# Loading the last 96 rows of w_out in two transfers of eight lanes

## The chip, the cores and the metric

The kernel runs on one core of a Trainium2 chip. The metric is the device time of one execution in microseconds (us). The core has five engines with queues of their own (TensorE, VectorE, ScalarE, GpSimd, SyncE) and sixteen DMA engines, which carry out the transfers that SyncE and ScalarE issue here.

## The reference

One decode step for a batch of four: a normalised input goes through attention over a cache of 4096 positions and, beside it, through a gated MLP; both results are added to x.

```python
# x: 4x1x640; k_cache, v_cache: 4x32x4096x128; wq: 640x4096; wo: 4096x640
# w_in: 640x1728; w_out: 864x640; all bfloat16
xn = layernorm(x)
q = (xn @ wq) per head                    # 32 heads of 128
p = softmax(q . k_cache * 128 ** -0.5)    # over 4096 positions
A = (p . v_cache) @ wo
z = gelu(xn @ w_in); z1, z2 = z[..., :864], layernorm(z[..., 864:])
B = (z1 * (w_sp * z2 + b_sp)) @ w_out
out = x + A + B
```

The two caches hold 268 MB; all that is read is 282 MB.

## The kernel before

The attention is cut into sixteen steps (NT = 16), one for eight heads of one batch element. A step reads one k tile and one v tile of 128 partitions x 64 KB, 8.4 MB each. In a step, VectorE multiplies the k tile by the query in place (L449) and folds it in half (L463), TensorE sums the products (L475), VectorE reduces them to scores (L486), ScalarE takes the exponentials (L542), and TensorE multiplies with v (L568).

Two k tiles and one v tile are in memory. The k load of step i + 2 is issued when step i has done with its tile; the v load of step i when the product of step i - 1 with v is done. From `tc.manual_schedule` on, the order of the work on TensorE, VectorE, ScalarE and SyncE is the order in which the code is written.

At the start SyncE issues, in this order, rows 0 to 767 of w_out (L109), wq (L114), w_in (L121), the last 96 rows of w_out (L123), and the first k tile (L139). ScalarE issues x, w_sp and b_sp. The weights of the MLP, w_in and w_out, share the buffer that later holds the v tiles, so the first v load (L145) waits until TensorE has used them (L216). The second k load takes the buffer of wq.

w_out has 864 rows. The first 768 lie on 128 partitions, six rows (7680 B) on each. The last 96 lie on sixteen partitions (TL = 16), again six rows on each (TK = 6). They are loaded by a loop over l, each turn of which fills TE partitions, at a stride of TL / TE. At the end, w_o comes in four transfers (L159) behind the last v tile, is multiplied (L216), and the result goes out (L736).

Of the kernel before, what the change touches and what calls it, by code (L numbers as in the profile page):

```python
# [17 lines left out]
def kernel(  # L18
# [48 lines left out]
    NFF = Fh // P  # L67
    TL = 16
    TK = (Fh - NFF * P) // TL
    TE = 4  # L70
    NFC = NFF + TK
    F0 = NFF * P
    TF = TL * TK
# [47 lines left out]
    nc.sync.dma_start(out=w_in_sb, in_=B_w_in.rearrange("(p c) n -> p c n", c=DC))  # L121
    for l in range(TL // TE):
        nc.sync.dma_start(  # L123
            out=w_out_sb[:TL, NFF:NFC, :].rearrange("(e l) k n -> e l (k n)", e=TE)[:, l],
            in_=B_w_out[F0:Fh].rearrange("(e l k) n -> e l (k n)", e=TE, k=TK)[:, l],
        )
# [642 lines left out]
```

## Time and profile before

| | |
|---|---|
| median of 3 runs | 662.66 us (662.63 to 662.77) |
| span of the profiled execution, first to last instruction | 661.07 us |
| median less this span | 1.59 us |
| DMA: packets, bytes, mean rate | 5712, 282.55 MB, 427 GB/s |
| VectorE busy | 491.6 us, 74% |
| TensorE busy | 295.4 us, 45% |
| ScalarE busy | 34.4 us, 5% |
| chain of waits by kind | DMA 51%, VectorE 37%, TensorE 9%, issue 2%, ScalarE 1% |

The profile gives times inside one execution, from its first to its last instruction; its own time as a whole is not given beside the span, so the median less the span stands for what lies around it. The chain of waits is followed back from the last instruction: at each step to what released it, or to the instruction before it on its engine. The DMA share is the mean busy share of the sixteen DMA engines. The trace also holds a record of each DMA packet: its start, its duration, its size and its queue.

### The profile page before, as it was taken

What the parts mean: (1) busy time and instruction counts of PE and PEld (TensorE: products, weight loads), DVE (VectorE), ACT (ScalarE), POOL (GpSimd) and SP (SyncE); (2) the same over time, 40 slices, a digit from 0 to 9 for tenths busy, and PEclk for the clock granted to TensorE, in tenths of its full rate; (3) what the DMA queues carried; (4) which work ended last, traced back from release to release, by engine and by line L of the source; (5) the groups of instructions that cost most, each with busy time, mean ns of one, the idle gap of its engine ahead of it and who ended that gap; (6) DMA issues with size and microseconds to landing.
All of it is one profiled execution on the core that took longest, in us unless ns stands there. A gap on an engine that the chain in (4) does not pass through costs nothing.

```text
span 661.1 us, 4720 instructions
## 1 busy us (share of the span) xinstructions
PE 295.4 (45%) x2099; PEld 127.9 (19%) x2099; DVE 491.6 (74%) x222; ACT 34.4 (5%) x94; POOL 2.1 (0%) x15
## 2 busy tenths in 40 slices
PE   0513464536426253552625344362634507263656
PEld 0301121212112021220202112120211202031223
DVE  1249999959597795959779569986959699695851
ACT  0300000000000000000000000000000000000000
POOL 1000000000000000000000000000000000000000
PEclk9756676876858687675868757787775768777688
DMA  8999999999999999999999999999999999999996
GB/s 377 456 428 444 428 417 441 429 436 441 436 420 433 432 429 445 440 421 432 424 436 441 440 425 432 420 441 436 437 428 437 425 432 429 440 432 437 432 406 275
DMA packets 5712, 282.55 MB, mean 427 GB/s; under 512 B 680, under 2 KB 812, under 8 KB 1084
## 3 DMA queue, kind: packets, MB, share of 16 engines
q1 hardware_dynamic: 5664, 282.24, 98.9%
q8 instruction: 16, 0.26, 0.2%
q14 instruction: 4, 0.03, 0.0%
q10 hardware_dynamic: 28, 0.01, 0.0%
HBM read 282.24 MB, written 0.01 MB: 427 GB/s over the span
## 4 chain that ended last, share of the span: by engine, by line
DMA 51%; DVE 37%; PE 9%; issue 2%; ACT 1%; SPq 0%; DVEq 0%; ACTq 0%
DMA k_nat<-in_A_k_cache_dram 47%; DVE k_nat L449 22%; DVE k_nat L463 11%; PE s_ps L475 8%; DMA wo<-in_A_wo_dram 4%; DVE s_sb L486 3%; DMA w_sb<-in_B_w_out_dram 1%; ACT p L542 1%; PE pv L568 1%; DVE m L495 1%; PE mT L500 0%; DVE nm L505 0%; DVE pm L553 0%; SPq L159 0%; PE out_ps L216 0%
## 5 line engine op out<-in xcount | busy, mean ns | idle before, releaser
L449 DVE TENSOR_TENSOR k_nat<-k_nat,qbc 128x16384 bf16<-128x16384 bf16 x32 | 278.0, 8688 | 97.8 <-DMA k_nat<-in_A_k_cache_dram 97.8
L475 PE MATMUL s_ps<-k_nat,ident 128*128 128x512 bf16 x528 | 184.8, 528 | 139.3 <-DVE k_nat L463 139.3
L463 DVE TENSOR_TENSOR k_nat<-k_nat 128x8192 bf16<-128x8192 bf16 x31 | 136.7, 4410 | 0.0
L475 PEld LDWEIGHTS <-ident 128*128 128x128 bf16 x528 | 65.3, 129 | 248.3 <-DVE k_nat L463 123.3
L500 PE MATMUL mT<-ident_f,m 128*1 128x128 f32 x16 | 5.9, 366 | 160.0 <-DVE m L495 160.0
L568 PE MATMUL pv<-v_nat,pm 128*32 128x512 bf16 x960 | 56.1, 387 | 0.8 <-DVE pm L553 0.8
L486 DVE TENSOR_REDUCE s_sb<-s_ps 128x128 f32<-128x1024 f32 x32 | 39.0, 1218 | 5.4 <-PE s_ps L475 5.4
L500 PEld LDWEIGHTS mT<-ident_f,m 128*1 128x1 f32 x16 | 1.3, 79 | 167.8 <-DVE m L495 156.2
L568 PEld LDWEIGHTS <-pm 128*32 128x32 bf16 x1024 | 27.1, 100 | 34.3 <-issue 8.5
L553 DVE TENSOR_TENSOR pm<-p,own_c 128x2048 bf16<-128x2048 bf16 x16 | 19.6, 1225 | 15.3 <-ACT p L542 15.3
L542 ACT ACTIVATE p<-s_sb,nb 128x256 bf16<-128x256 f32 x16 | 8.1, 508 | 394.1 <-DVE nb_h L524 394.1
L591 PE MATMUL o_ps<-e,pick 128*32 128x128 f32 x128 | 17.0, 276 | 11.2 <-ACT e L578 11.2
L591 PEld LDWEIGHTS o_ps<-e,pick 128*32 128x32 f32 x128 | 12.7, 109 | 18.7 <-ACT e L578 18.7
L578 ACT COPY e<-pv 128x512 f32<-128x512 f32 x16 | 9.4, 586 | 68.1 <-PE pv L568 60.6
L287 DVE COPY qT<-qT_ps 128x64 bf16<-128x64 bf16 x2 | 0.4, 224 | 15.5 <-PE qT_ps L282 15.5
L516 PE MATMUL nb_ps<-nm,ones_row 1*128 1x8 f32 x32 | 9.2, 359 | 6.0 <-DVE nm L505 6.0
L505 DVE TENSOR_REDUCE nm<-mT 1x8 f32<-1x128 f32 x16 | 4.5, 279 | 7.5 <-PE mT L500 7.5
L516 PEld LDWEIGHTS nb_ps<-nm,ones_row 1*128 1x128 f32 x32 | 7.7, 298 | 10.6 <-DVE nm L505 9.9
L271 PE MATMUL q_ps<-wq,xnT_r 128*32 128x512 bf16 x40 | 4.3, 609 | 11.2 <-DMA wq<-in_A_wq_dram 11.2
L443 ACT CAST qbc<-qbc_ps 128x128 bf16<-128x128 f32 x16 | 4.3, 266 | 92.3 <-PE qbc_ps L435 92.3
L608 PE MATMUL den<-ones_col,acc_h 128*32 128x1 f32 x8 | 1.0, 194 | 16.6 <-DVE acc_h L601 16.6
L495 DVE TENSOR_REDUCE m<-s_sb 128x1 f32<-128x256 f32 x16 | 6.7, 420 | 0.5
(92 smaller groups left out, 70.7 us busy)
## 6 DMA issues: line engine op xcount, KB each, us to landing
wq<-in_A_wq_dram SPq DMA_DIRECT2D x1, 5120.0 KB, 16.3
wo<-in_A_wo_dram SPq DMA_DIRECT2D x1, 2560.0 KB
w_sb<-in_B_w_in_dram SPq DMA_DIRECT2D x1, 2160.0 KB, 20.9
wo<-in_A_wo_dram SPq DMA_DIRECT2D x1, 1760.0 KB
w_sb<-in_B_w_out_dram SPq DMA_DIRECT2D x1, 960.0 KB
wo<-in_A_wo_dram SPq DMA_DIRECT2D x1, 640.0 KB, 25.5
k_nat<-in_A_k_cache_dram SPq DMA_DIRECT2D x16, 39.6
v_nat<-in_A_v_cache_dram SPq DMA_DIRECT2D x15, 33.7
```

The source lines that it names most:

```text
L449: nc.vector.tensor_tensor(out=part(i, u), in0=part(i, u), in1=qbcs[i][:, None, :].to_broadcast([P, UC, Dh]), op=ALU.mult,)
L463: nc.vector.tensor_tensor(out=t[:, :, 0:HD2], in0=t[:, :, 0:HD2], in1=t[:, :, HD2:Dh], op=ALU.add)
L475: nc.tensor.matmul(out=sums_ps[i][:, c : c + SC], lhsT=ident[:], rhs=t[:, c : c + SC, g * RW : (g + 1) * RW], start=(g == 0), stop=(g == n ...
L486: nc.vector.tensor_reduce(out=scores[i][:, u * UC : (u + 1) * UC], in_=sums_ps[i][:], axis=AX.X, op=ALU.add,)
L495: nc.vector.tensor_reduce(out=m1[:], in_=scores[i][:], axis=AX.X, op=ALU.max)
L500: nc.tensor.transpose(out=mT[:], in_=maxes[i][:], identity=ident_f[:])
L516: nc.tensor.matmul(out=nb_ps[:], lhsT=ones_row[:], rhs=maxes[i][:], start=True, stop=True)
L542: nc.scalar.activation(out=probs[i][:], in_=scores.pop(i)[:], func=ACT.Exp, bias=maxes.pop(i)[:], scale=scale_qk, accum_out=accs[hg][:, b ...
L553: nc.vector.tensor_tensor(out=pm[:], in0=probs.pop(i)[:] .rearrange("p (n c) -> p n c", c=CB)[:, :, None, :] .to_broadcast([P, NB, HT, CB] ...
L568: nc.tensor.matmul(out=pvs[i][j * GW : (j + 1) * GW, :], lhsT=pm[:, n, :, :].rearrange("p h c -> p (h c)"), rhs=v_nat[:, n * CB : (n + 1) ...
L578: nc.scalar.copy(out=es[i][:], in_=pvs.pop(i)[:].rearrange("p (c d) -> p c d", d=Dh))
L591: nc.tensor.matmul(out=o_ps[hg // NG][own_rows(hg), :], lhsT=pick[:, c, GW - HT - HT * b : 2 * GW - HT - HT * b], rhs=e[:, c, :], start=(b ...
```

## The change

TE goes from 4 to 8. The loop that loads the last 96 rows of w_out runs TL / TE times: two turns in place of four. Each transfer fills eight partitions (0, 2, ..., 14 and then 1, 3, ..., 15) in place of four (0, 4, 8, 12, and so on). Bytes, places in memory and all later instructions are the same; the program has 48 transfers in place of 50.

```diff
@@ -67,7 +67,7 @@
     NFF = Fh // P
     TL = 16
     TK = (Fh - NFF * P) // TL
-    TE = 4
+    TE = 8
     NFC = NFF + TK
     F0 = NFF * P
     TF = TL * TK
```

The loop that it acts on:

```python
    for l in range(TL // TE):
        nc.sync.dma_start(
            out=w_out_sb[:TL, NFF:NFC, :].rearrange("(e l) k n -> e l (k n)", e=TE)[:, l],
            in_=B_w_out[F0:Fh].rearrange("(e l k) n -> e l (k n)", e=TE, k=TK)[:, l],
        )
```

## The prediction

> **What bounds the kernel now.** I read the page first, for the share of the DMA engines, then busy time by stretch, then the chain of waits, then SyncE's queue, and last the trace's record of single DMA packets.
>
> The page's rows on queues (packets, MB, share of 16 engines' span) show what fills the time:
>
> ```profile
> q1 hardware_dynamic: 5664, 282.24, 98.9%
> q8 instruction: 16, 0.26, 0.2%
> q14 instruction: 4, 0.03, 0.0%
> ```
>
> The sixteen DMA engines are at work for 98.9% of the span. Busy time by stretch (the last two numbers of a row are the DMA share and GB/s) shows that they have no gap from start to end:
>
> ```profile
> 6.00:22.00 16.00, 4.82 (x50) 2.00 (x48) 1.09 (x5) 0.77 (x2) 0.71 (x4) 1.00 1.05 454
> 22.00:43.00 21.00, 7.30 (x137) 6.10 (x135) 4.04 (x23) 4.60 (x10) 0.00 (x0) 0.57 1.01 434
> ...
> 120.00:630.00 510.00, 231.11 (x1504) 96.79 (x1506) 400.26 (x153) 21.24 (x65) 0.00 (x0) 0.71 1.00 433
> ```
>
> So the bound is the bytes through the DMA engines: 282.24 MB at 433 GB/s is 652 us, and the rest is the start before the first packet and the end after the last w_o row. The chain of waits (start, us, what) begins like this:
>
> ```profile
> 0.73 4.59 DMA w_sb<-in_B_w_out_dram
> 5.34 0.58 SPq L123
> 5.92 0.04 issue
> 5.96 37.25 DMA k_nat<-in_A_k_cache_dram
> ```
>
> It says that the fourth tail transfer of w_out waited for the main w_out load, and that the first k load was issued only behind it. It must not be read as 5.96 us lost: of the 37.25 us until that load landed, most is the queue ahead of it (w_out, wq and w_in). The packet records have the first k packet at 21.84 us, 15.9 us after the issue, on an engine that had just ended its share of w_in.
>
> SyncE's queue in order of time and its longest wait there:
>
> ```profile
> 2.16 3.76 SPq L123 DMA_DIRECT2D w_sb<-in_B_w_out_dram  x4
> 5.96 16.17 SPq L139 DMA_DIRECT2D k_nat<-in_A_k_cache_dram  x2
> 35.70 0.33 SPq L145 DMA_DIRECT2D v_nat<-in_A_v_cache_dram  x1
> 76.89 0.33 SPq L139 DMA_DIRECT2D k_nat<-in_A_k_cache_dram  x1
> ```
> ```profile
> SPq L123 <- DMA w_sb<-in_B_w_out_dram: 1.2, 1, 1.2
> ```
>
> **Why the fourth tail waited.** The trace names the semaphore of every DMA: eight of them, taken in turn (x, w_out, wsp, bsp, wq, w_in, tail 0, tail 1, and from the start again: tail 2 with x, tail 3 with w_out), and a DMA waits until the one eight places before it has landed.
>
> **The change, part by part.** (1) *Two issues fewer.* On SyncE's queue the four cost 0.73 + 0.59 + 0.58 + 0.58 us, and the 1.2 us wait lies between the third and fourth. Two remain, about 1.4 us with their gaps, so the first k load is issued near 3.6 us in place of 5.96, 2.4 us earlier. Cover: 8.4 MB of w_out, wq and w_in lie ahead of it until 21.8 us. The cover would have to shrink by over 15 us before this counted. Worth: 0.
>
> (2) *All later transfers move two places on in the eight semaphores.* The first k load now follows x (landed by 2.2 us), the second follows w_out (landed by 5.3; this load waits for the q projection until 21.81 anyway), the first v load follows wsp, the next k and v loads follow bsp, wq, w_in and the two tails, all landed by 24 us, before the first of these is issued at 35.7. From there on the predecessor is four k/v pairs back. The w_o and output transfers have the same predecessors as before, since both moved by two. Worth: 0, and no new wait. POOL's queue and ACT's are not moved past; ACT's two small loads keep their places.
>
> (3) *The same 16 rows on other DMA engines.* This is the only part that touches the bound. Packets that follow one another without a gap on one engine form chains, sixteen of them. Each tail transfer leaves four packets of 7680 B and four completion writes; x, with four lanes, also has four writes, a one-lane load one, a 128-lane load sixteen. So lanes up to sixteen are one engine each, and the sixteen tail packets, at 22.10 to 23.10 us, lie on the same four chains, four each, 0.29 us apart. At the first k packet twelve chains start within 0.33 us of each other and those four 1.44 to 1.55 us behind the first; their own phase is some 0.3 us, so the tails cost them 4 x 0.287 = 1.15 us. With eight lanes there are two packets on each of eight chains: the old four gain 0.57 us, four others lose 0.57 us, and eight see nothing.
>
> Does it count? The kernel ends with the chain that ends last, since the last w_o piece needs all sixteen. By the packet records, w_o ends on them thus:
>
> - tail chains: 654.7, 654.9, 655.6, 656.7 us
> - the chains that fetch instructions (the 16 KB packets of queue q8, in turn over eight chains; each puts its chain back by 1.0 us, and the packet after it by 0.5): 655.1, five from 656.5 to 656.7, then 657.06 and 657.12
> - the four others: 653.3, 653.5, 653.6, 654.6
>
> The chain of waits has w_o landed at 657.23. It is set by two fetching chains (657.06 and 657.12), not by a tail chain: each of those fetched twice, 3.0 us, more than the 1.15 us of tails. Taking 0.57 us off the tail chains leaves the maximum where it is: 0. Adding 0.57 us to the four others leaves them at 655.2 or less: 0. If instead the four that lose are among the fetching ones, the end moves by up to +0.57. Bounds of this part: 0 and +0.57; a gain is excluded by the two fetching chains unless their own delays change (below). I take 0: the eight fetching chains avoid all four tail chains, which looks like a split in halves, with the first eight lanes on the half without them.
>
> The Trainium skill (DMA: Bandwidth & Descriptors, on why a DMA raises its semaphore by 16) says that such a DMA uses as many engines as the largest number up to 16 that divides its outermost size, and the lowest-numbered ones. The trace agrees with the first half (4 writes for 4 lanes); which number a chain has no record here shows. It doesn't alter the sum.
>
> (4) *The tail lands earlier.* Last tail packet at 23.1 us, on a chain that now has two fewer: 22.5. TensorE's w_in product (L317) waited 0.9 us for it and starts some 0.5 us sooner, and with it the release of the weight buffer, so the first v load goes at about 35.1 in place of 35.70. The queue then holds k until 61 us. Worth: 0. The first k load's landing is set by a fetching chain too (its fetch at 29.2 us leaves it 1.62 behind, against 1.55 for the latest tail chain), so VectorE starts its first product when it did.
>
> Sum on the profiled execution: 0 + 0 + 0 + 0 on a span of 661.07 us. The median of three, 662.66, lies 1.6 us above that span, and I carry this over: 662.7. A measurement of this kernel can tell about 0.2%, or 1.3 us, from no change, so every bound of (3) lies inside it.
>
> **Rivals.**
>
> *Slower: the four new chains are ones that fetch.* Place: the ends above. If four of the eight fetching chains get two tail packets each, and one of the latest two is among them, the end moves to 657.6 to 657.7: +0.5 to +0.57, 663.2. It decides as soon as a chain that ends after 656.55 gets the packets. For it: eight of the twelve possible chains fetch. Against: the split above. 0.2.
>
> *Faster, a little: a disturbed stretch does not return.* At 80 to 88 us, at the start of the third k load, packets that elsewhere take 2.42 us took up to 3.21, and two fetching chains lost about 0.75 us each for good; they are among the latest. If that hangs on the engines' phase, which the change shifts on eight chains, it may be gone. Then the next latest, 656.69, sets the end: -0.43, 662.2. It may as well hit others. 0.1.
>
> *Faster: the chain of waits taken at its word.* If the first k load really came 2.4 us sooner and all behind it too: 660.3. Against it: DMA share 1.05 and 1.01 in the two stretches above; nothing to start sooner on. 0.04.
>
> *Faster: a fixed price per transfer.* If every transfer held the engines for its issue time, two fewer would save 2 x 0.58 = 1.2 us: 661.5. Against it: the packets of the four tails follow each other at 0.29 us with no gap. 0.02. The Trainium skill (same page, rules for kernel authors) advises to coalesce small transfers, since those under 64 KB pay mostly overhead; its fixed cost of about 2.0 us would, as an estimate, make this 4 us, and the gapless packets speak against it here.
>
> *Slower by more: the queue runs dry at the third k load.* It is issued at 76.89 and its first packet runs at 79.80; the shortest way from issue to packet seen here is 1.0 us (0.73 to 1.76), so 1.9 us of slack. If the first k load landed more than 1.9 us later, the excess would be lost in full; 3.2 us later would make 664.0. Nothing in the sum delays it by more than 0.57. 0.03.
>
> **How the numbers follow.** The forecast (nothing that counts) has 0.61. Range: from 662.0, a little under the case without the disturbed stretch, to 663.3, over the +0.57; this leaves out about 0.1 of the listed cases and some room for errors in the reading of chains. Faster by over 0.2% is the case taken at its word and half of the fixed price; slower is the dry queue: 0.05 and 0.03, and 0.92 within.
>
> **What would show it.** After the change: L123 x2 on SyncE's queue, no wait on w_out there, the first k load issued near 3.6 us and still landing near 43; sixteen tail packets as eight pairs on eight chains; DMA share 1.00 from 6 to 630; w_o landing at 657.2 and output behind it as before. A landing of w_o at 657.7 with 16 KB fetches on the new tail chains is the first rival. I am wrong if the queue shows a gap, if w_o lands over 1.3 us elsewhere, or if the k loads' rate of 433 GB/s moves.

## The result and the profile after

The changed kernel is slower by a little: 663.79 us (663.44 to 664.23, 21 runs) against 662.61 (662.44 to 662.95, 21 runs), +1.18 us; the ratio is 1.0018, with an interval of 1.0011 to 1.0024. The forecast was 662.7 with a range to 663.3. The profiled execution has a span of 662.07 us.

The page's row on SyncE's queue (packets, MB, share), and busy time by stretch (stretch, length, then PE, PEld, DVE, ACT and POOL, granted clock, and as the last two DMA share and GB/s):

```profile
q1 hardware_dynamic: 5664, 282.24, 98.8%
```
```profile
6.00:22.00 16.00, 4.64 (x46) 1.75 (x44) 1.09 (x5) 0.58 (x1) 0.71 (x4) 1.00 1.00 430
22.00:43.00 21.00, 7.80 (x143) 6.33 (x139) 4.05 (x23) 4.79 (x10) 0.00 (x0) 0.59 1.07 449
120.00:630.00 510.00, 232.29 (x1490) 96.85 (x1492) 400.07 (x152) 21.21 (x65) 0.00 (x0) 0.71 1.00 433
```

The DMA engines are busy throughout, at 433 GB/s in the long stretch as before. The rates of the first two stretches (454 and 434 GB/s before) differ only because a packet counts in the stretch in which it starts: seven first k packets of 65536 B started ahead of 22.00 us before, one does now. A loss of 1.2 us in 650 can't be seen in a share; nor can a stall, since an engine whose packet takes longer counts as busy. SyncE's queue and the start of the chain of waits (start, us, what):

```profile
2.17 1.46 SPq L123 DMA_DIRECT2D w_sb<-in_B_w_out_dram  x2
3.67 18.81 SPq L139 DMA_DIRECT2D k_nat<-in_A_k_cache_dram  x2
35.99 0.33 SPq L145 DMA_DIRECT2D v_nat<-in_A_v_cache_dram  x1
77.74 0.33 SPq L139 DMA_DIRECT2D k_nat<-in_A_k_cache_dram  x1
```
```profile
2.99 0.64 SPq L123
3.63 0.04 issue
3.67 40.30 DMA k_nat<-in_A_k_cache_dram
44.00 8.70 DVE k_nat L449
```

The first k load is issued 2.3 us sooner and lands at 43.97 (3.67 + 40.30), which is 0.76 us later than before (5.96 + 37.25 = 43.21). So most of what was lost was lost before 44 us. At the end of the chain w_o lands at 658.12, against 631.75 + 25.48 = 657.23; the first line here is that of the kernel before, the other three are those of the changed one:

```profile
631.75 25.48 DMA wo<-in_A_wo_dram
```
```profile
632.72 25.40 DMA wo<-in_A_wo_dram
658.12 0.04 issue
658.16 0.68 PE out_ps L216 x20
```

The rest comes from the records of single packets, joined into sixteen chains, one for each DMA engine, as in the prediction. Columns: how long the first k packet (65536 B) took on chains without tail rows; how long a tail packet (7680 B) took; when the last write of w_o, a small one that reports its end, began.

| kernel | first k packet, us | tail packet, us | last w_o write, us |
|---|---|---|---|
| before | 2.42 | 0.29 | 657.12 |
| after | 2.88 to 2.94 | 0.29 to 0.53 | 658.02 |

Tail packets that ended by 22.61 us took 0.29; those that ended later, up to 23.14, took longer and longer, and the k packets behind them were still too long. Tail and first k packet together, fifteen chains lost 0.46 to 0.53 us and one 0.70, the eight that carry no tail row too. Below, this is called the stretch: the packets of all chains take longer for a while. And the two chains that end last (657.96 and 658.02) are tail chains that each fetched two 16 KB blocks of instructions. So there are two candidate parts: a stretch on all chains, and tails on chains that fetch. The experiments take them apart. Each gives its time against the runs of before on the same chip, then the ratio and its interval.

### The profile page after: what moved, and what is told of

The parts are those of the page before. It is cut to its first block, busy times and chain, and to the rows that moved or that the text cites. A ratio compares the mean times of both kernels' runs of the same rounds, so it can differ in the third digit from the quotient of the medians.

```text
span 662.1 us, 4717 instructions
## 1 busy us (share of the span) xinstructions
PE 295.8 (45%) x2099; PEld 127.9 (19%) x2099; DVE 491.6 (74%) x222; ACT 34.4 (5%) x94; POOL 2.1 (0%) x15
## 4 chain that ended last, share of the span: by engine, by line
DMA 51%; DVE 37%; PE 9%; issue 2%; ACT 1%; SPq 1%; DVEq 0%; ACTq 0%
DMA k_nat<-in_A_k_cache_dram 47%; DVE k_nat L449 22%; DVE k_nat L463 11%; PE s_ps L475 8%; DMA wo<-in_A_wo_dram 4%; DVE s_sb L486 3%; ACT p L542 1%; PE pv L568 1%; DVE m L495 1%; PE mT L500 0%; DVE nm L505 0%; DVE pm L553 0%; SPq L123 0%; SPq L159 0%; PE out_ps L216 0%
```

## Experiments: where the stretch comes from

**Two small loads behind the tails (e1_filler).** The changed kernel, with the old number of transfers:

```diff
+    fill = const.tile([1, 2], BF16, name="fill")
+    for l in range(2):
+        nc.sync.dma_start(out=fill[:, l : l + 1], in_=B_w_out[0:1, l : l + 1])
```

> The eight-lane transfers kept, and behind them two loads of 2 bytes into an unused tile, so that the program has 50 transfers again, with the wait for w_out, and the first k load is issued near 5.9 us as before the change. Theory A (where the rows land): in the changed kernel the second half of the tail packets took 0.34 to 0.53 us in place of 0.29, and the first k packet on all sixteen chains took 2.7 to 3.1 us in place of 2.42, because eight lanes at a time write into the same four groups of four partitions (0-3, 4-7, 8-11, 12-15) that the four-lane transfers fill one lane each. Then this stretch comes again here, w_o lands near 658.0 and the time is that of the changed kernel, 663.6 to 664.0 us. Theory B (the early issue): the stretch comes from the first k load being queued 2.3 us sooner. Then the first k packets take 2.42 us here and the time falls by some 0.45 us, to 663.1 to 663.4.

663.56 against 662.68 us (1.0013, 1.0004 to 1.0022). The first k packet took 2.84 to 2.86 us on the chains without tails, the tail packets up to 0.51, and w_o was last written at 657.93. The first k load was issued at 5.67 us here, so the stretch is there without the early issue; theory B loses.

**The early issue alone (e6_early).** The kernel before, with two loads replaced:

```diff
-    nc.scalar.dma_start(out=wsp_bf[:], in_=B_w_sp[0:1, 0:1])
-    nc.scalar.dma_start(out=bsp_bf[:], in_=B_b_sp[0:1].rearrange("(a b) -> a b", a=1))
+    nc.gpsimd.memset(wsp_bf[:], 0.0)
+    nc.gpsimd.memset(bsp_bf[:], 1.0)
```

> The four-lane transfers of before the change, but w_sp and b_sp are set to constants in place of being loaded (these two values are left out), so that the program has 48 transfers, no tail transfer waits for w_out, and the first k load is issued near 4.8 us in place of 5.96. Theory A: the early issue costs nothing, the first k packets take 2.42 us, and the time is that of before, 662.5 to 662.8. Theory B: the early issue stretches the first k packets by 0.46 us: 663.0 to 663.2.

662.51 against 662.68 us (0.9999, 0.9990 to 1.0008): no change. The first k load was issued at 4.86 us, and all first k packets but one took 2.42 us (one 2.55). That is 1.1 us earlier than before, not the 2.3 of the changed kernel; two runs further down, with this load issued at 3.81 and at 2.45 us, have first k packets of 2.42 us too. The issue order and the turn of the semaphores cost nothing that these runs can tell, as steps 1 and 2 of the prediction said.

**Four adjacent partitions (e2_contig4).** The kernel before, with the other order of lanes, on both sides of the transfer:

```diff
-            out=w_out_sb[:TL, NFF:NFC, :].rearrange("(e l) k n -> e l (k n)", e=TE)[:, l],
-            in_=B_w_out[F0:Fh].rearrange("(e l k) n -> e l (k n)", e=TE, k=TK)[:, l],
+            out=w_out_sb[:TL, NFF:NFC, :].rearrange("(l e) k n -> e l (k n)", e=TE)[:, l],
+            in_=B_w_out[F0:Fh].rearrange("(l e k) n -> e l (k n)", e=TE, k=TK)[:, l],
```

> Four transfers of four lanes as before the change, but of adjacent partitions: 0-3, then 4-7, 8-11, 12-15, so that all four lanes of a transfer lie in one group of four partitions. Same engines, same bytes, same queue, same waits as before. Theory A: if a group takes rows only at one engine's rate, the 16 packets need up to 16 x 0.29 = 4.6 us in place of 1.15 on the four tail chains; these lie up to 3.4 us further back, so w_o lands on them at up to 660.2 in place of 656.7 (657.12 on the last chain), and if the k packets of the other chains are held up as in the changed kernel, by over 0.46 us: 663.5 to 666. Theory B, and any theory that goes only by the number of engines and transfers: nothing changes against before, 662.6.

663.54 against 662.68 us (1.0014, 1.0005 to 1.0022). Theories that go by numbers alone lose: engines, bytes, queue and waits are those of before. But the size in theory A was wrong: the tail packets took 0.29 to 0.60 us and were through in 2.0 us, not 4.6, and the other chains lost only 0.05 us at the first k packet (2.43 to 2.49). The tail chains fell back by 0.7 us. These four do not end last, and in the profiled run one other chain lost 1.2 us more at 80 us and a second 0.3 (see the last section), so where this kernel's 0.86 us goes is only partly seen.

**Eight lanes into groups of their own (s2_own).** Rows, lanes and transfers of the changed kernel, other partitions (an unused part of the weight buffer); the product with the tail is left out. The new lines, in their place:

```diff
+    nc.gpsimd.memset(w_out_sb[:TL, NFF:NFC, :], 0.0)
+    spare = w_sb[0:32, 20480 : 20480 + TK * D].rearrange("(e l) n -> e l n", e=8)
+    for l in range(2):
         nc.sync.dma_start(
+            out=spare[:, l],
+            in_=B_w_out[F0:Fh].rearrange("(e l k) n -> e l (k n)", e=8, k=TK)[:, l],
         )
```

> The same two transfers of eight lanes with the same rows and 7680 B a lane as in the changed kernel, and the same early issue of the first k load, but each lane goes to a group of four partitions of its own (partitions 4e and 4e + 1 for lane e, in an unused part of the weight buffer). The product with the tail is left out (it works on zeros), so the loaded rows go unused. Theory A (the stretch comes from where the rows land): tail packets at 0.29 us, first k packets at 2.42; the new tail chains still carry 0.57 us and two of them fetch: 662.9 to 663.3 us. Theory C (it comes from the reading side: eight rows at a stride of 15360 B read at once): tail packets to 0.5 us, first k packets at 2.7 to 3.1: 663.5 to 664.0.

662.97 against 662.69 us (1.0003, 0.9994 to 1.0011). Every first k packet took 2.42 us, every tail packet 0.29. Its chain of waits:

```profile
3.81 39.40 DMA k_nat<-in_A_k_cache_dram
...
631.99 25.51 DMA wo<-in_A_wo_dram
```

The first k load lands at 43.21 (3.81 + 39.40), to the hundredth as before the change, and w_o at 657.50. The reading side is the same as in the changed kernel, and so are lanes, bytes and early issue, so theory C loses: the stretch hangs on where the rows land.

**Four lanes to far partitions (s4_far4), and to near ones (s8_mid4).** The same edit with `e=4`, four transfers, and partitions 64 to 79 or 16 to 31 of `w_sb` in place of 0 to 31:

> Four transfers of four lanes on the same engines as before the change, each lane in a group of four partitions of its own, but at partitions 64 to 79 of the unused part of the buffer, where at that time other engines write their k rows. The product with the tail is left out. Theory A1 (two engines that write one group hold each other up, and with them all chains): tail packets or the k packets beside them take longer than 0.29 and 2.42 us, and the time rises by 0.2 to 0.5 us over that of before: 662.8 to 663.2. Theory A2 (only lanes of one transfer in one group hold each other up): no stretch, 662.4 to 662.7.

> The four-lane transfers of before on the same engines, each lane in a group of its own, but at partitions 16 to 31 in place of 0 to 15. The product with the tail is left out. Theory A1 (a group has an engine that fills it in the 128-lane loads; a row that another engine writes there holds up both, and with them all sixteen chains): the first k packets take about 3.4 us on all chains as they did with partitions 64 to 79, and the time is 663.6 to 664.0. If only the far half (64 and up) is costly, no stretch: 662.5 to 662.9.

663.85 against 662.69 us (1.0017, 1.0008 to 1.0026) and 663.86 against 662.73 (1.0017, 1.0008 to 1.0026). In both, the first k packet took 3.42 to 3.50 us on the twelve chains without tails, 1.0 us more than 2.42, and tail packets took up to 0.59. The chain of waits of the far one:

```profile
6.06 38.66 DMA k_nat<-in_A_k_cache_dram
44.72 0.02 issue
...
633.17 24.96 DMA wo<-in_A_wo_dram
```

Number of lanes, engines and transfers are those of before, no two lanes of a transfer share a group of four partitions, and yet the first k load lands 1.5 us later than before. So theory A as first put (only lanes of one transfer in one group) is too narrow, and A2 with it. A1 has the direction right: each group of four partitions has an engine that fills it in the 128-lane loads, and rows that another engine writes there hold up all sixteen. Its time for the far partitions, 662.8 to 663.2, was too low; the one for the near partitions, put down after that, held. The far half is not special.

The Trainium skill gives the map: in DMA: Bandwidth & Descriptors, section on the descriptor swizzle, engine 8 x (p >> 6) + ((p >> 2) & 7) writes partition p of a 128-partition transfer, and by the section on why a DMA raises its semaphore by 16 a transfer of few lanes takes the lowest-numbered engines. By it engines 0 to 3 fill partitions 0-3, 4-7, 8-11 and 12-15, which is where the old four lanes put their rows, engine by engine; the new eight lanes put engine 1's rows into engine 0's group, those of 2 and 3 into 1's, and so on. No packet record names its engine. The placements tried, those further down included, sort by this map into own groups and others (second column: what the first k packet took beyond 2.42 us on chains without tails):

| tail lanes, by the map | first k packet longer by, us | tail packet, us |
|---|---|---|
| own groups: kernel before, e6_early, s2_own, e4_own8, s11_six8, s12_six4 | 0 to 0.02; in three profiles one chain 0.13 to 0.16 | 0.29 (0.15 for half the bytes) |
| engines 0-7 into groups of 0-3: changed kernel, e1_filler, a1_after | 0.42 to 0.64 | 0.29 to 0.57 |
| engines 0-15 into groups of 0-3: e5_one16 | 0.27 to 0.87 (all chains have a tail) | 0.29 to 0.93 |
| engines 0-3 into groups of 4-7 or 8-11: s8_mid4, s4_far4 | 1.0 to 1.1 | 0.29 to 0.59 |
| engines 0-3, all four into one of their groups at a time: e2_contig4 | 0.01 to 0.07 | 0.29 to 0.60 |

Only own groups leave all packets as they were. The last row departs from A1: there the tail packets were long, and the other chains were hardly held up. The Trainium skill says of copies between cores that a saturated write port holds back other engines (same page, on back-pressure in remote DMA). That fits the rows with a stretch, but no run here shows the port itself.

**One transfer of sixteen lanes (e5_one16).** `TE = 16` in the kernel before:

> One transfer of sixteen lanes, so that each of the sixteen chains has one packet of the tail (0.29 us) and four lanes lie in each group of four partitions. By number of engines alone: all chains 0.29 us later, the fetching ones included, so the end is 0.29 us later than before: 662.9. Theory A: the packets of the sixteen chains and the first k packets are stretched at least as in the changed kernel (0.46 us on all chains), beside the 0.29 us: 663.3 to 664.0.

663.87 against 662.69 us (1.0019, 1.0010 to 1.0028). First k packets up to 3.29 us (most 0.7 to 0.8 over 2.42), tail packets up to 0.93. The count of engines alone (662.9) loses; one transfer is as slow as the two of the changed kernel.

**32 partitions, eight lanes (e4_own8).** `TL = 32`, `TE = 8`:

> The 96 rows on 32 partitions, three rows (3840 B) each, in four transfers of eight lanes at a stride of four partitions, so that each lane of a transfer lies in a group of four of its own. The number of transfers, the wait and the issue near 5.9 us are as before the change; the eight tail chains get four packets of 3840 B each, 0.57 us, as in the changed kernel. TensorE has three tail steps in place of six. Theory A: no stretched packets, so the 0.46 us on all chains is gone, but two of the new tail chains still fetch instructions and end last: 0.57 us on those. That is about 0.45 us below the changed kernel: 663.1 to 663.5. If the fetching chains were not the cause of the rest, the time would be that of before, 662.6; if eight lanes by themselves stretch the packets, it stays at 663.8.

663.13 against 662.68 us (1.0005, 0.9997 to 1.0014). First k packets 2.42 to 2.43 us, tail packets 0.149 for their 3840 B: no stretch, with eight lanes and the whole computation. By the two parts it was to be 663.1 to 663.5, and it is. But the interval reaches down to no change, so this run alone does not show the second part; and its profiled execution (663.66) is the slowest of its eleven, with up to 1.1 us lost on several chains at 80 us.

## Experiments: which chains carry the tails

**No tail at all (e7_notail).** The loop of L122 is replaced by a memset of zeros:

> The last 96 rows of w_out are not loaded (zeros stand in for them; their product is left out); all else is as before the change, with the first k load issued near 2.6 us. If the end is set by the fetching chains and the four tail chains have time to spare, as read from the packets of before, the 1.15 us of the tails were free: 662.1 to 662.7. If the tails of before had cost time, it falls by up to 1.15 us: 661.5.

662.77 against 662.69 us (1.0001, 0.9992 to 1.0010), w_o last written at 656.92; the first k load was issued at 2.45 us. The four-lane tails of the kernel before cost nothing that can be told (interval -0.5 to +0.7 us): 1.15 us on four chains were hidden.

**More on the same chains, first try (s6_own8x4, s7_own4x2).** The tail rows again and again into own groups, in eight transfers:

```diff
+    for r in range(4):   # two rounds with four lanes
+        c0 = 16384 + r * TK * D
         # ... spare = w_sb[0:32, c0 : ...] with e=8 (0:16 with e=4), then the loop over l as in s2_own
```

> The eight-lane transfers into groups of their own, four times over (eight transfers): each of the eight tail chains carries eight packets, 2.3 us in place of 0.57. The product with the tail is left out and the loaded rows go unused. Theory A with the fetching chains (two of the eight fetch and would end last by themselves): the end moves by the other 1.7 us in full against the run with two transfers into own groups (662.97): 664.5 to 664.9 us. If the end does not hang on these chains, it stays at 662.7 to 663.2.

> The four-lane transfers into groups of their own, twice over (eight transfers again): each of the four tail chains carries eight packets, 2.3 us, as each of the eight chains does in the run beside it. The product with the tail is left out. These four chains fetch no 16 KB packets. Theory A with the fetching chains: they have 0.4 to 2.4 us to spare beyond their 1.15 us in the kernel before, so most of the extra 1.15 us is free and only the chain with two 8 KB packets may come last, at 657.9: 662.7 to 663.5 us. If it went by the load on any chain, it would be that of the eight-lane run beside it, 664.5 or more.

665.85 and 665.75 against 662.73 us (1.0048, 1.0035 to 1.0060; 1.0046, 1.0032 to 1.0060). A miss of the experiment: with eight transfers the last one takes the semaphore of w_in and waits until w_in has landed. SyncE's queue of the eight-lane run:

```profile
2.16 21.09 SPq L127 DMA_DIRECT2D w_sb<-in_B_w_out_dram  x8
23.30 0.91 SPq L143 DMA_DIRECT2D k_nat<-in_A_k_cache_dram  x2
```

The first k load is issued at 23.3 us, after the engines have emptied the queue; its first packets run from 24.4 in place of 21.9. Both kernels lose the gap, and nothing is learnt of chains.

**Second try (s9_wide8, s10_wide4).** Two transfers of eight lanes (four of four) with 24 (twelve) rows a lane:

> Two transfers of eight lanes into groups of their own, as in the run at 662.97 us, but 24 rows (30720 B) a lane in place of six: each of the eight tail chains carries 2.3 us in place of 0.57, with the same number of transfers and the same early issue. The product with the tail is left out and the loaded rows go unused. If two of these chains fetch and end last, the other 1.7 us shows in full: 664.4 to 664.9 us. If the end does not hang on these chains, 662.7 to 663.2.

> Four transfers of four lanes into groups of their own, as before the change, but twelve rows (15360 B) a lane: each of the four tail chains carries 2.3 us in place of 1.15, with the number of transfers and the wait of before. The product with the tail is left out and the loaded rows go unused. With the fetching chains as cause: these four chains fetch no 16 KB packets and have 0.4 to 2.4 us to spare, so the time rises by 1.0 us at most, where the one with two 8 KB packets comes last, 662.7 to 663.7. If load counts on whichever chain it lies, it comes out with the eight-lane run beside it, 664.4 or more.

671.88 and 671.61 against 662.72 us (1.0138, 1.0124 to 1.0152; 1.0132, 1.0117 to 1.0148). A miss again, for another reason. SyncE's queue and two stretches of the eight-lane run:

```profile
2.37 0.64 SPq L142 DMA_DIRECT2D k_nat<-in_A_k_cache_dram  x1
22.81 1.46 SPq L126 DMA_DIRECT2D w_sb<-in_B_w_out_dram  x2
...
87.57 0.33 SPq L142 DMA_DIRECT2D k_nat<-in_A_k_cache_dram  x1
```
```profile
70.00:78.00 8.00, 3.72 (x11) 1.23 (x9) 8.00 (x3) 1.55 (x2) 0.00 (x0) 0.71 1.19 516
78.00:90.00 12.00, 6.21 (x16) 2.15 (x16) 12.00 (x3) 0.00 (x0) 0.00 (x0) 0.64 0.37 137
```

The tails stood behind the first k load in the queue and were issued only at 22.81 us, after w_in had landed; why they stood there is not known. So the MLP and everything behind it came late, and the third k load was issued at 87.57 us in place of 76.89. From 80 us on most engines had nothing to do (share 0.37 from 78 to 90 us, against 0.98 before) and lost some 8 us. This is the prediction's last rival, the dry queue at the third k load, with its price: all of the delay beyond the slack, and from issue to packet 1.0 us here too.

**Third try (s11_six8, s12_six4).** Six transfers of 7680 B a lane into own groups, with eight or with four lanes:

```diff
+    for r in range(6):
+        c0 = 20480 + r // 2 * TK * D        # r // 4 with four lanes
+        spare = w_sb[0:32, c0 : c0 + TK * D].rearrange("(e l) n -> e l n", e=8)   # 0:16, e=4
         # ... then one transfer: lanes r % 2 (r % 4 with four lanes) of the tail rows into spare
```

> Six transfers of eight lanes into groups of their own, three times the two of the run at 662.97 us: 1.72 us on each of the eight tail chains in place of 0.57. The last of them takes the semaphore of b_sp (landed by 8.5 us) and the first k load that of wq (17.2), so all are queued before w_in ends at 21.8. The product with the tail is left out and the loaded rows go unused. If two of these chains fetch and end last, the other 1.15 us shows in full: 663.9 to 664.4 us. If the end does not hang on these chains: 662.7 to 663.2.

> Six transfers of four lanes into groups of their own: the same 1.72 us, on the four tail chains of before (1.15 there), with the same queue as the eight-lane run beside it. The product with the tail is left out and the loaded rows go unused. With the fetching chains as cause: these four fetch no 16 KB packets and have 0.4 to 2.4 us to spare, so at most the one with two 8 KB packets comes last, by 0.2: 662.5 to 663.1 us. If load counts on whichever chain it lies: 663.9 or more.

664.35 (663.96 to 664.59) against 662.59 us for eight lanes (1.0024, 1.0014 to 1.0034) and 663.15 (662.77 to 664.03) for four (1.0009, 1.0000 to 1.0018). Same queue, same 1.72 us on every loaded chain, every tail packet 0.29 us, no stretch (2.42 to 2.43; one chain 2.55 in the four-lane run): 1.2 us apart by which chains are loaded. The eight-lane run also moves 184 KB more, but at 433 GB/s these are 0.43 us if all engines share them, and less than the difference. Start of the chain of waits with eight lanes:

```profile
1.21 16.39 DMA wq<-in_A_wq_dram
17.61 26.18 DMA k_nat<-in_A_k_cache_dram
```

The late issue of the k load (17.61, behind wq) is well ahead of the 21.8 us at which the engines get to it. With eight lanes w_o ends late on two chains, both with tails: 658.20 and 658.19, where no other ends after 657.39. With four it ends at 657.09. Against two transfers into own groups (662.97), the further 1.15 us of the eight-lane run shows in full (+1.38). The four-lane run is a little over its forecast of 662.5 to 663.1.

**The changed kernel and the kernel before once more (a1_after, e0_before).**

> The changed kernel once more, beside the others. The first k packets at 2.7 to 3.1 us on all chains, w_o landing last on two tail chains with two 16 KB packets each, near 658.0. By the two parts (0.46 us on all chains, and 0.3 us as in the run into own groups) the time would be 663.4 to 663.6; by its own runs 663.6 to 664.0.

> The kernel before, profiled once more. If the disturbed stretch at 80 to 88 us belongs to this kernel, packets of up to 3.2 us come again there on several chains; if it is chance, the third k load runs at 2.42 us a packet. The time is 662.4 to 663.1 either way, w_o landing between 656.6 and 657.2, last on chains that fetch.

663.71 against 662.72 us for the changed kernel (1.0014, 1.0005 to 1.0023), first k packets 3.0 to 3.06 us on most chains, last write of w_o at 657.96. The kernel before: 662.68 us in one run, last write of w_o at 656.82, and of the disturbed stretch at 80 us there are left 0.1 us on two chains. So its own first profile was somewhat late: from 656.82 to 658.02 is 1.20 us, and the change's loss is 1.18.

## Why the prediction was wrong

**Steps 1 and 2 held.** Two issues fewer, the wait for w_out gone, the first k load issued at 3.67 us (3.6 was forecast), all semaphores free in time: worth nothing, as the early issue alone showed (662.51). The rival that took the chain of waits at its word was wrong for the reason given.

**Step 3 failed in two places.** The first is the price of a tail packet. I took 0.29 us from the row of before for all sixteen, and two per chain. That row was for lanes that write the partitions their own engine fills. The new lanes do not: their packets took up to 0.53 us, and all chains, with or without tails, lost about half a microsecond (0.46 to 0.53, one 0.70). The prediction looked at which engines read the rows and never at which partitions they write. No forecast or rival had this. It is what put the time outside the range: the same two eight-lane transfers into own groups took 662.97 us.

The second is the choice of 0 between 0 and +0.57. "A split in halves" was a guess, and wrong: by the records after, two of the four new tail chains fetch 16 KB blocks. The first rival, given 0.2, was right in place: the same load per chain costs more on eight chains, four of them new, than on the old four alone (664.35 against 663.15 us). Its size, +0.5 to +0.57, is less sure: 0.3 us by the times of the run into own groups, whose interval includes no change, and 0.6 by the last write of w_o (657.40 against 656.82). The records of before could not tell which chains the new lanes would take, so the bound of eight in twelve should have weighed more than the look of a split: of four chains drawn blindly from the twelve, at least one fetches in 494 draws of 495, and one of the latest two is among them in 0.58 of the draws.

Sum against the second profile of before: the latest fetching chains ended their first k packet at 24.6 us there; after the change the latest tail chain that fetches does so at 25.84. Of these 1.2 us, 0.57 are the two tail packets and 0.52 the stretch (0.23 on the second tail packet, 0.29 on the k packet); the small rest lies before the tails.

**Step 4 had the sign wrong.** The last tail packet ended at 23.14 us, not 22.5, TensorE's w_in product started at 24.25 in place of 23.85, and the first v load went at 35.99, not 35.1. Without the stretch of 0.23 us that packet would have ended at 22.90, so the gain to be had was 0.2 us and not 0.6, and the stretch took it. It cost nothing by itself, as forecast; the third k load still came in time.

**The other rivals.** The disturbed stretch at 80 us did go in the changed kernel, which as forecast helps by some 0.3 us on the profiled execution, but it comes and goes in the kernel before as well. A fixed price per transfer has no support: without any of the four tails the time was 662.77 against 662.69 us.

The remaining difference between the runs of the changed kernel (+1.18 and +0.99) and of the one with fillers (+0.88) is inside their intervals and stays open. No version ran faster than the kernel before by more than its interval.

## What to carry to other kernels

Where DMA engines are busy throughout, a transfer over few partitions is not only bytes: count which engines carry it and which partitions they write, and keep each lane in the group of four partitions that its engine fills in the 128-lane loads; that was the only placement here that held up no other packet. Read the end from the chain that ends last, not from the mean share: load on engines with time to spare is free (1.15 us on four chains cost nothing), and the same bytes spread evenly can land on those without. A bound that the records leave open should keep the weight of its count, whatever pattern it seems to make.

## What the runs showed of the hardware that I had not expected

- Rows written into another engine's group of partitions can slow all sixteen engines, not only the two: sixteen packets of 7680 B from four engines cost every chain 1.0 to 1.1 us, whether into partitions 16 to 31 or 64 to 79. Where the four engines that own partitions 0 to 15 wrote into each other's groups, the tail packets took up to 0.60 us and the other chains lost no more than 0.07. Why the reach differs was not settled. One difference is that in this last case all four owners of the groups were themselves at the tails; no run tests whether that is it.
- A fetch of 16 KB of instructions sets one engine back by 1.0 us (0.94 to 1.11) and its next packet by 0.5 (0.46 to 0.55), although 16 KB are 0.6 us at the rate of k packets (65536 B in 2.42 us). Eight engines take these in turn, twice each in this kernel, and so end up to 3 us behind the rest.
- At the third k load (77 to 88 us) some chains lose 0.1 to 1.2 us in some runs (most in the run with 32 partitions) and none in others, the kernel before included. What it is was not found.
